# Two of four pairs of heads of the third half transposed by DMA instead of TensorE, with three reorderings around it

## The chip, the cores and the metric

The kernel runs on one core of a Trainium2 chip. The core has a matrix engine (TensorE, PE in the profile; its weight loads are listed apart as PEld), a vector engine (VectorE, DVE), an engine for activation functions and copies (ScalarE, ACT), a general engine (GpSimd, POOL) and an engine that here only issues transfers (SyncE, SP). Transfers run on 16 DMA engines; SP and POOL each keep a queue of them. The metric is the time of one execution on the device in microseconds, less is better. It is given as the median of several runs.

## The reference

The computation is attention with a limited window, followed by a gated feed-forward layer. `q`, `k` and `v` are 4 batches x 8 heads x 768 positions x 64 values, all float32.

```python
scores = scale * np.matmul(q, k.transpose(0, 1, 3, 2))
is_global = pos[None, :] < n_global                    # 8
is_local = (rel >= 0) & (rel < n_local)                # 96
dist = np.where(is_global & ~is_local, n_local, np.abs(rel))
bias = -slopes[:, None, None] * dist
a = softmax(np.where(is_global | is_local, scores + bias, -1e9))
x = np.matmul(a, v)            # then 3072 tokens x 512 (8 heads side by side)
out = (np.maximum(x @ w_gate, 0.0) * (x @ w_val)) @ w_out
```

A query sees the first 8 positions and the last 96 up to itself. `w_gate` and `w_val` are 512 x 1536, `w_out` is 1536 x 512. So there are two products of 512 x 1536 per token and one of 1536 x 512, and these are most of the arithmetic.

## The kernel before, in words

**Tiling.** The work is cut into 8 halves: half `s` is batch `s // 2` and half `s % 2` of its 768 positions, so 384 queries (`QH`). "Third half" in this document is `s = 2`, the first half of the second batch. In each half the 8 heads form four pairs `p` (`HP`), two heads of 64 values filling 128 rows. The keys of a batch form 7 tiles of 128 columns: 8 global keys and 120 others, so that one product yields scores against both. A pair's scores of one half fill three groups of columns. The feed-forward layer has 12 blocks of 128 columns (`N_FC`); its weights lie in SBUF in three groups of four blocks: `wg[0..2]`, `wv[0..2]`, and `wo_sb` for `w_out`.

**Steps of a half.** Keys and queries come with 128 positions on the rows of SBUF, and the scores need the 64 values there, so they are transposed first. Then come scores (PE), exponential (ACT), multiplication with a mask that holds the bias and the window (DVE), the product with v (PE), the logarithm and exponential that make a reciprocal (ACT, tiles `lnd` and `rcp`) and the multiplication into `xT` (DVE). The feed-forward follows, for each block `fc`: a gate product of four matmuls (one per quarter `dc` of the 512 inputs), a relu on ACT (`grelu`), a value product of four matmuls, and on DVE the product of both into `ht`. The output products read `ht` and `wo_sb`.

**Three ways of transposing.** Halves 0 and 1 are transposed by TensorE: `piece_t` (L288) multiplies with the identity, six or twelve matmuls at L299 per pair, into a PSUM bank; `piece_copy_k` (L304, copies at L278 to L280) and a copy of the queries bring them to SBUF. For half 1 the load itself casts to bfloat16 (`kc`, `qc`). Halves 3 to 7 use transfers: `early_pieces` (L378) has POOL cast keys and queries into `kc`/`qc` (`piece_cast2`), SP issue three DMA transposes each (`piece_x`, one per third `n` of the positions, all four pairs at once), and POOL put the keys into their tiles (`piece_order`, three copies per pair). Half 2 stands between: POOL casts (`cast(2, p, P, P)`, L979, from the loaded `ks`, `qs`), TensorE transposes, DVE makes three copies for the keys and ACT one for the queries (`T2_piece`, L982).

**The order of the work.** [...] The first part, up to the end of half 1's attention, is written out line by line. After it, `weave` (L813) emits a list of feed-forward items and puts other pieces between them: a piece with place 0.55 is emitted once 55% of the items' weight is out, and `spread` (L808) lays a list evenly between two places. `F0[2*i]` is the gate of block `i` of half 0 and `F0[2*i+1]` its value product. The first weave (L988) holds the blocks of half 1 and the rest of half 0's second group, with the third half's transposes among them; it runs from about 32.6 to 47.0 us. The second (L994) holds the last group of blocks, the output products of halves 0 and 1, the attention of the third half, the transposes of half 3 and the sums of `w_out` (`sums_wo`, DVE); it runs from 47.0 to 75.7 us.

**Buffers and queues.** Feed-forward products take turns in 3 PSUM banks (`ff_ps`), scores and the third half's transposes in 3 (`qk_ps`), products with v in 2 (`av_ps`). POOL issues the loads of weights and of v and those of `kc`/`qc`; SP issues the loads of later keys and queries, the copies that spread v's global rows over the seven tiles (`spread_v_globals`, L144), the DMA transposes and the stores. Weights and the third half's keys and queries are requested together at L923 to L926 in this order: `wg[1]`, `wv[1]`, `wg[2]`, `wv[2]`, keys, queries, `wo_sb`.

```python
weave(f1_1[G[0]] + f1_0[G[1]][4:] + f1_1[G[1]],
      ...
      spread(T2, 0.55, 0.95))
```

Of the kernel before, what the change touches and what calls it, by code (L numbers as in the profile page):

```python
# [16 lines left out]
def kernel(  # L17
# [12 lines left out]
    nc = tc.nc  # L30

    B, H, S, D = q.shape
# [6 lines left out]
    HP = H // 2  # L39
    QH = S // 2  # L40
    NN = 3
# [13 lines left out]
    for half in range(2):  # L55
# [33 lines left out]
    kNb = [const.tile([128, HP, QH], BF16, name=f"kN{i}") for i in range(2)]  # L89

    qT2 = [qTb[1].rearrange("d p e t -> d (p e t)")[:, i * HP * QH : (i + 1) * HP * QH].rearrange(
        "d (p t) -> d p t", p=HP) for i in range(2)]
    qc = [const.tile([128, NN, DM], BF16, name=f"qc{i}") for i in range(2)]
    kc = [const.tile([128, NN, DM], BF16, name=f"kc{i}") for i in range(2)]
# [16 lines left out]
    qs_of, ks_of = {}, {}  # L111

    def load_qk(s, h0, h1, eng=nc.sync):
        b, half = divmod(s, 2)
        if s not in qs_of:
            qs_of[s] = stage.tile([128, H, NN * D], FP32, name="qs")
            ks_of[s] = stage.tile([128, H, NN * D], FP32, name="ks")
        for src, dst in ((k, ks_of[s]), (q, qs_of[s])):
            eng.dma_start(
                out=dst[:, h0:h1, :],  # L120
                in_=src[b, h0:h1, half * QH : (half + 1) * QH, :].rearrange(
                    "h (p n) d -> p h (n d)", n=NN))
# [17 lines left out]
    def load_v_globals(b):  # L140
        nc.gpsimd.dma_start(out=v_dst(b, 0, NG, 0),
                            in_=v[b, :, 0:NG, :].rearrange("h p d -> p h d"))

    def spread_v_globals(b, j0=1, j1=NT):  # L144
        for j in range(j0, j1):
            nc.sync.dma_start(out=v_dst(b, 0, NG, j), in_=v_dst(b, 0, NG, 0))
# [5 lines left out]
    def load_v(b, j, r0=0, r1=KT):  # L152
        n = min(r1, S - KT * j) - r0
        nc.gpsimd.dma_start(  # L154
            out=v_dst(b, NG + r0, NG + r0 + n, j),
            in_=v[b, :, KT * j + r0 : KT * j + r0 + n, :].rearrange("h p d -> p h d"))
# [5 lines left out]
    def load_v_half(s):  # L162
        b, half = divmod(s, 2)
        if half == 0:
            load_v_globals(b)
            spread_v_globals(b)
        for j in range(4) if half == 0 else range(4, NT):
            load_v(b, j)

    def load_w(dst, src, f0, f1):  # L170
        nc.gpsimd.dma_start(out=dst, in_=src[:, f0:f1].rearrange("(c p) f -> p c f", p=128))

    def load_w_group(i):
        load_w(wg[i], moe_w_gate, i * GW * 128, (i + 1) * GW * 128)
        load_w(wv[i], moe_w_val, i * GW * 128, (i + 1) * GW * 128)
# [91 lines left out]
    def put_keys(copy, copy_small, kt, src, half):  # L267

        tk = src.rearrange("d (n p) -> d p n", n=NN)

        def put(j0, j1, p0, r0, r1):
            o = kt[:, j0:j1, r0:r1].rearrange("d j (p n) -> d j p n", n=NN)
            np_ = (r1 - r0) // NN
            i_ = tk[:, p0 : p0 + (j1 - j0) * np_, :].rearrange("d (j p) n -> d j p n", j=j1 - j0)
            return o, i_

        if half == 0:
            copy(*put(0, 3, 0, NG, 128))  # L278
            copy_small(*put(3, 4, 120, NG, NG + 24))
            copy_small(kt[:, :, 0:NG], kt[:, 0:1, NG : 2 * NG].to_broadcast([128, NT, NG]))  # L280
        else:
            copy(*put(4, 6, 32, NG, 128))
            copy_small(*put(3, 4, 0, NG + 24, 128))
            copy_small(*put(6, 7, 112, NG, NG + 48))
# [3 lines left out]
    def piece_t(s, p, pool=av_psum, name="av_ps", apart=False):  # L288
        for i in (1, 0):
            if i == 1 or apart:  # L290
                tp = pool.tile([128, 512], FP32, name=name)
                tp = tp[:, 0:QH].bitcast(BF16).rearrange("d (i t) -> d i t", i=2)
            tp_of[s, p, i] = tp[:, i, :]
            for n in range(NN):
                for e in range(2 if s == 1 else 1):
                    r = slice(64 * e, 64 * e + 64) if s == 1 else slice(0, 128)
                    src = (qk16[s, i][:, 2 * p + e, n * D : (n + 1) * D] if s == 1
                           else cast_of[s, p][:, i, n])
                    nc.tensor.matmul(tp[r, i, n * 128 : (n + 1) * 128],  # L299
                                     lhsT=src, rhs=ident, is_transpose=True,  # L300
                                     start=((i == 1 or apart) and n == 0),
                                     stop=((i == 0 or apart) and n == NN - 1))

    def piece_copy_k(s, p):  # L304
        b, half = divmod(s, 2)
        put_keys(nc.vector.tensor_copy, nc.vector.tensor_copy, kT[b % 2][p], tp_of[s, p, 1], half)

    def piece_copy(s, p):
        piece_copy_k(s, p)
        piece_copy_q(s, p)  # L310

    def piece_copy_q(s, p, copy=nc.vector.tensor_copy):
        for e in range(2):
            r = slice(64 * e, 64 * e + 64)
            copy(qTb[s % 2][r, p, e, :], tp_of[s, p, 0][r, :])
# [50 lines left out]
    def piece_cast2(s, p, dst, src):  # L366
        nc.gpsimd.tensor_copy(  # L367
            dst[s % 2].rearrange("t n (h d) -> t h n d", d=D)[:, 2 * p : 2 * p + 2],
            src[s][:, 2 * p : 2 * p + 2, :].rearrange("t e (n d) -> t e n d", n=NN))

    def piece_x(dst, src, n):
        nc.sync.dma_start_transpose(out=dst[:, :, n * 128 : (n + 1) * 128], in_=src[:, n])

    def piece_order(s, p):
        b, half = divmod(s, 2)
        put_keys(nc.gpsimd.tensor_copy, nc.gpsimd.tensor_copy, kT[b % 2][p], kNb[s % 2][:, p], half)
# [9 lines left out]
    def piece_qk(s, p, g, later=None):  # L386
        b, half = divmod(s, 2)
        kt = kT[b % 2][p]
        qd = qTb[s % 2][:, p].rearrange("d e (n p) -> d e n p", n=NN)
        bank = banks_of_half[half][g]  # L390
        cols = sum(2 * NN * w for _, _, w, _ in bank)
        ps = qk_psum.tile([128, 512], FP32, name="qk_ps")
        es = es_pool.tile([128, 480], BF16, name="es")
        c = 0
        for j, a, w, m in bank:
            n_ = 2 * NN * w
            nc.tensor.matmul(ps[:, c : c + n_], lhsT=kt[:, j, :],
                             rhs=qd[:, :, :, a : a + w], start=True, stop=True)
            c += n_
        nc.scalar.activation(es[:, 0:cols], ps[:, 0:cols], AF.Exp, bias=0.0, scale=scale)  # L400
        if later is None:
            piece_mask(s, p, bank, es)
        else:
            later.append(lambda: piece_mask(s, p, bank, es))
# [88 lines left out]
    def piece_mul_wide(s, p):  # L493
        if s not in xT_of:
            xT_of[s] = xt_pool.tile([128, N_DC, QH], BF16, name="xT")
        nc.vector.tensor_tensor(xT_of[s][:, p, :], av_of[s, p][1][:, 0:QH], av_of[s, p, "r"], op=ALU.mult)
# [311 lines left out]
    def spread(items, first, last, n=None):  # L808

        n = n or len(items)  # L810
        return [(first + (i + 0.5) / n * (last - first), f) for i, (_, f) in enumerate(items)]
# [22 lines left out]
    F0 = [f for _, f in f1_0]  # L834
# [86 lines left out]
    piece_biased(1, 0)  # L921
    load_v(0, 3, 24)
    load_w_group(1)  # L923
    load_w_group(2)
    load_qk(2, 0, H, nc.gpsimd)
    load_w(wo_sb, moe_w_out, 0, DM)  # L926
    for f in gate[0:3]:
        f(0, LAST)
    for f in gate[0:3]:
        f(LAST, N_DC)  # L930
    piece_t(1, 2)
    piece_t(1, 3)
    masks = {p: [] for p in (1, 2)}
    for g in range(3):
        piece_qk(1, 1, g, masks[1])
    piece_copy(1, 2)
    gate[3]()
    piece_copy(1, 3)
# [25 lines left out]
    piece_inverse_wide(1, 2)  # L964
    piece_ln_wide(1, 3)
    piece_mul_wide(1, 2)
    F0[9]()
    piece_inverse_wide(1, 3)
    piece_mul_wide(1, 3)
    F0[10]()  # L970
    F0[11]()
    for p in range(HP):
        nc.gpsimd.memset(kT[1][p][:, 3, 32:128].bitcast(mybir.dt.uint32), 0)
# [1 line left out]
    nc.gpsimd.memset(vbuf[1][:, NT - 1, :].bitcast(mybir.dt.uint32), 0)  # L975
    for j in range(NT):
        fill_ones(nc.gpsimd, 1, j)
    for p in range(HP):
        cast(2, p, P, P)  # L979
    load_v_half(2)  # L980

    def T2_piece(p):  # L982
        piece_t(2, p, *QKB, apart=True)
        piece_copy_k(2, p)
        nc.scalar.copy(qT2[0][:, p], tp_of[2, p, 0])

    T2 = [(0.0, lambda p=p: T2_piece(p)) for p in range(HP)]
    weave(f1_1[G[0]] + f1_0[G[1]][4:] + f1_1[G[1]],  # L988
          [(0.05 + 0.06 * j, lambda j=j: fill_ones(nc.vector, 0, j)) for j in range(NT)],
          [(0.1 + 0.2 * i, lambda h=h: setup_mask(h)) for i, h in enumerate((0, 1, 6, 7))],  # L990
          [(0.6, lambda: load_qk(3, 0, H)), (0.6, lambda: load_v_half(3))],
          spread(T2, 0.55, 0.95))
    sums_wo = [(0.0, f) for i in (0, 3) for f in weight_sums(i, i + 3)]
    weave(f1_0[G[2]] + f1_1[G[2]] + f2_0 + f2_1,  # L994
          spread(attention_pieces(2), 0.02, 0.86, 30), spread(early_pieces(3), 0.1, 0.76),
          spread(sums_wo, 0.08, 0.4))

    for c in range(2, NHALF):
        placed = []
# [43 lines left out]
```

The softmax here doesn't subtract the row's maximum and nothing guards it: scores larger than these inputs give would overflow.

## Time and profile before

| What | Value |
|---|---|
| Median of 7 runs | 237.44 us (237.13 to 237.76) |
| The profiled execution | 237.74 us, of which 236.0 us is its span |
| PE busy | 228.8 us (97%) |
| DVE busy | 186.9 us (79%) |
| ACT busy | 146.1 us (62%) |
| POOL busy | 88.8 us (38%) |
| Read and written in HBM | 28.38 MB and 6.29 MB |

The span runs from the first to the last instruction; the time of the execution also has what lies before and after it. Busy shares are averages over stages with different limits, so they are read stage by stage. Here are the stretches that matter, from the profile's table of windows (for each engine the busy time in us; "DMA share" is the mean load of the 16 engines, where a value over 1 means that packets overlap on an engine):

| Stretch, us | PE | DVE | ACT | POOL | DMA share | GB/s |
|---|---|---|---|---|---|---|
| 0 to 23 | 19.62 | 17.46 | 19.84 | 20.63 | 1.33 | 178 |
| 23 to 32.6 | 9.54 | 7.05 | 8.26 | 6.53 | 1.36 | 202 |
| 32.6 to 47 (first weave) | 14.40 | 10.73 | 8.51 | 7.41 | 1.21 | 250 |
| 47 to 75.7 (second weave) | 28.70 | 24.72 | 16.71 | 14.87 | 1.02 | 158 |
| 75.7 to 200 | 124.08 | 103.15 | 82.05 | 39.39 | 0.55 | 118 |
| 200 to 236 | 32.49 | 23.78 | 10.72 | 0.00 | 0.13 | 45 |

The TensorE clock that was granted is 1.00 throughout. PE's ends are modelled, so its busy time says that it always had work queued, not that each matmul ran at its peak.

### The profile page before, as it was taken

To read this page: it belongs to the slowest core of one execution; us is meant where nothing else is said; L and a number is where in the kernel's file an instruction comes from. 1 tells how busy PE (TensorE), PEld (TensorE's weight loads), DVE (VectorE), ACT (ScalarE), POOL (GpSimd) and SP (SyncE) were. 2 spreads that over 40 slices of the span, in tenths; PEclk is the share of its full clock that TensorE was granted. 3 is DMA by queue.
4 is the path that set the end of the run, shared out by engine and by line. 5 is a ranking of instruction groups with operands and counts; after the bars stand their busy time and mean duration, and the time that the engine had idled before them with its cause. 6 is when DMAs were issued, how large, how long until landed. Compare 5 with 4: busy or idle time off the path is not lost.

```text
span 236.0 us, 5509 instructions
## 1 busy us (share of the span) xinstructions
PE 228.8 (97%) x2021; PEld 158.0 (67%) x2021; DVE 186.9 (79%) x466; ACT 146.1 (62%) x321; POOL 88.8 (38%) x191
## 2 busy tenths in 40 slices
PE   7889999999999999999999999999999999999994
PEld 3675666656678666856688666856679566865683
DVE  6868767769988789786999789886899779773784
ACT  7979875667624887467842787567842687624310
POOL 8998902942583066406580066405330000000000
PEclk9999999999999999999999999999999999999999
DMA  6999999998359856856397764846422200020005
GB/s 186 184 158 183 205 253 292 178 120 263 75 142 185 253 162 92 52 166 215 90 83 118 239 172 90 53 139 223 87 44 89 92 0 3 0 92 0 1 3 178
DMA packets 71420, 30.43 MB, mean 129 GB/s; under 512 B 47745, under 2 KB 70785, under 8 KB 71393
## 3 DMA queue, kind: packets, MB, share of 16 engines
q0 software_dynamic: 34896, 10.27, 38.9%
q1 hardware_dynamic: 36496, 19.82, 29.6%
q8 instruction: 16, 0.26, 0.5%
q14 instruction: 12, 0.09, 0.1%
HBM read 28.38 MB, written 6.29 MB: 147 GB/s over the span
## 4 chain that ended last, share of the span: by engine, by line
PE 86%; DVE 3%; POOL 3%; DMA 3%; ACT 2%; issue 1%; POOLq 0%; DVEq 0%; ACTq 0%
PE ff_ps L748 52%; PE ff_ps L634 20%; PE av_ps L431 6%; DMA kc<-in_q_dram 3%; PE ff_ps L781 2%; PE av_ps L515 2%; PE qk_ps L515 2%; POOL vbuf L154 1%; DVE obuf L647 1%; PE qk_ps L299 1%; PE av_ps L468 1%; ACT es L400 1%; ACT es L359 1%; PE qk_ps L468 1%; ACT grelu L757 0%
## 5 line engine op out<-in xcount | busy, mean ns | idle before, releaser
L757 ACT ACTIVATE grelu<-ff_ps 128x384 bf16<-128x384 f32 x96 | 46.7, 490 | 51.8 <-PE ff_ps L748 38.6
L748 PE MATMUL ff_ps<-xT,wv 128*128 128x384 bf16 x384 | 77.9, 326 | 0.0
L748 PE MATMUL ff_ps<-xT,wg 128*128 128x384 bf16 x384 | 77.8, 326 | 0.0
L764 DVE TENSOR_TENSOR ht<-ff_ps,grelu 128x384 f16<-128x384 f32 x96 | 53.3, 557 | 27.2 <-PE ff_ps L748 22.9
L748 PEld LDWEIGHTS <-wv 128*128 128x128 bf16 x384 | 36.0, 98 | 23.9 <-issue 1.4
L748 PEld LDWEIGHTS <-wg 128*128 128x128 bf16 x384 | 36.4, 97 | 21.2 <-issue 0.5
L647 DVE TENSOR_TENSOR obuf<-ff_ps,obuf 128x512 f32<-128x512 f32 (+1 forms) x46 | 27.6, 603 | 5.3 <-ACT rcp L446 2.2
L367 POOL CAST kc<-ks 128x384 bf16<-128x384 f32 x20 | 10.2, 552 | 54.1 <-DMA ks<-in_k_dram 54.1
L536 DVE TENSOR_TENSOR es<-es,m_all 128x432 bf16<-128x432 bf16 (+3 forms) x108 | 30.3, 324 | 0.2 <-ACT es L524 0.2
L453 DVE TENSOR_TENSOR xT<-av_ps,rcp 64x384 bf16<-64x384 f32 x48 | 26.5, 553 | 4.7 <-ACT rcp L446 4.0
L440 ACT ACTIVATE lnd<-av_ps 64x384 f32<-64x384 f32 x48 | 23.3, 485 | 11.1 <-PE av_ps L431 10.3
L524 ACT ACTIVATE es<-qk_ps 128x432 bf16<-128x432 f32 (+2 forms) x54 | 27.7, 532 | 0.0
L154 POOL DMA_DIRECT2D vbuf<-in_v_dram x29 | 24.8, 870 | 0.3 <-DVE hsum L630 0.3
L431 PEld LDWEIGHTS <-vbuf 128*128 128x128 bf16 x216 | 18.3, 98 | 4.7 <-DVE xT L453 0.4
L431 PE MATMUL av_ps<-es,vbuf 128*128 128x216 bf16 (+4 forms) x216 | 21.4, 226 | 0.0
L634 PEld LDWEIGHTS <-ht 128*128 128x128 f16 x198 | 18.6, 97 | 3.5 <-DVE ht L764 0.5
L634 PEld LDWEIGHTS <-hsum 128*128 128x128 f16 x192 | 18.5, 98 | 2.1
L634 PE MATMUL ff_ps<-wo_sb,ht 128*128 128x256 f16 x132 | 18.5, 272 | 0.2 <-DVE ht L764 0.2
L634 PE MATMUL ff_ps<-wo_sum,hsum 128*128 128x256 f16 x144 | 17.2, 273 | 0.0
L446 ACT ACTIVATE rcp<-lnd 128x384 f32<-128x384 f32 x24 | 12.6, 524 | 0.7
L524 ACT ACTIVATE es<-av_ps 128x432 bf16<-128x432 f32 (+2 forms) x18 | 9.5, 528 | 1.8 <-PE qk_ps L515 1.8
L515 PEld LDWEIGHTS <-kT 64*128 64x128 bf16 x216 | 6.6, 94 | 5.9 <-issue 3.8
(130 smaller groups left out, 264.2 us busy)
## 6 DMA issues: line engine op xcount, KB each, us to landing
out_dram<-obuf SPq DMA_DIRECT2D x22, 256.0 KB
ks<-in_k_dram SPq DMA_DIRECT2D x5, 768.0 KB
qs<-in_q_dram SPq DMA_DIRECT2D x5, 768.0 KB
vbuf<-in_v_dram POOLq DMA_DIRECT2D x23, 120.0 KB, 4.7
wv<-in_moe_w_val_dram POOLq DMA_DIRECT2D x3, 512.0 KB, 10.1
wo_sb<-in_moe_w_out_dram POOLq DMA_DIRECT2D x1, 1536.0 KB, 21.7
wg<-in_moe_w_gate_dram POOLq DMA_DIRECT2D x2, 512.0 KB, 10.0
ks<-in_k_dram SPq DMA_DIRECT2D x4, 192.0 KB
```

The source lines that it names most:

```text
L154: nc.gpsimd.dma_start(out=v_dst(b, NG + r0, NG + r0 + n, j), in_=v[b, :, KT * j + r0 : KT * j + r0 + n, :].rearrange("h p d -> p h d"))
L431: nc.tensor.matmul(av3[:, :, a : a + w], lhsT=vb[:, j, z0 : z0 + 128], rhs=es[:, c : c + NN * w].rearrange("k (n p) -> k n p", n=NN), star ...
L440: nc.scalar.activation(ln[o0 : o0 + 64], av[d0 : d0 + 64, 0:QH], AF.Ln, bias=0.0, scale=1.0)
L453: nc.vector.tensor_tensor(xT_of[s][r, p, :], av_of[s, p, e][r, 0:QH], av_of[s, p, "r"][r], op=ALU.mult)
L515: nc.tensor.matmul(banks[e][:, c : c + NN * w], lhsT=kT[b % 2][p][r, j, :], rhs=q3[:, :, a : a + w], start=True, stop=True)
L524: nc.scalar.activation(es[:, 0:cols], ps[:, 0:cols], AF.Exp, bias=0.0, scale=scale)
L536: nc.vector.tensor_mul(e4, e4, mk)
L634: nc.tensor.matmul(ps[:, c0 : c0 + DH], lhsT=lhs(i), rhs=rhs(i), start=(i == 0), stop=(i == NP - 1), skip_group_check=True)
L647: add = lambda o, x, y: nc.vector.tensor_tensor(o, x, y, op=ALU.add)
L748: nc.tensor.matmul(st[key][:, 0:QH], lhsT=w_of(w, dc, fc), rhs=xT_of[c][:, dc, :], start=(dc == 0), stop=(dc == N_DC - 1))
L757: nc.scalar.activation(gr, psg[:, 0:QH], AF.Relu, bias=0.0, scale=1.0)
L764: nc.vector.tensor_tensor(ht[:, fc, :], psv[:, 0:QH], st["r", fc], op=ALU.mult)
```

## The change

The change has six parts.

1. The third half's keys and queries are requested before `wg[2]` and `wv[2]` instead of after them.
2. The scores of half 1's pair 1 are put ahead of the transposes of half 1's pairs 2 and 3.
3. In the last part before the first weave, gate 5 of half 0 (`F0[10]`) comes ahead of value product 4 (`F0[9]`).
4. The third half's pairs 2 and 3 are cast by POOL into `kc[0]` and `qc[0]` (their half of the columns), transposed by six DMA transposes of two pairs' width on SP's queue (`piece_x` has a new parameter for the first pair), and put into their key tiles by POOL (`piece_order`), behind the issue of the v loads. Pairs 0 and 1 stay with `cast` and TensorE.
5. `T2` holds two pieces instead of four, spread over places 0.65 to 0.95 instead of 0.55 to 0.95.
6. The sums of `w_out` begin at place 0.1 instead of 0.08.

```diff
-    def piece_x(dst, src, n):
-        nc.sync.dma_start_transpose(out=dst[:, :, n * 128 : (n + 1) * 128], in_=src[:, n])
+    def piece_x(dst, src, n, p=0):
+        nc.sync.dma_start_transpose(out=dst[:, p:, n * 128 : (n + 1) * 128], in_=src[:, n, 128 * p :])
...
     load_w_group(1)
+    load_qk(2, 0, H, nc.gpsimd)
     load_w_group(2)
-    load_qk(2, 0, H, nc.gpsimd)
     load_w(wo_sb, moe_w_out, 0, DM)
...
-    piece_t(1, 2)
-    piece_t(1, 3)
     masks = {p: [] for p in (1, 2)}
     for g in range(3):
         piece_qk(1, 1, g, masks[1])
+    piece_t(1, 2)
+    piece_t(1, 3)
...
     piece_mul_wide(1, 2)
-    F0[9]()
+    F0[10]()
     piece_inverse_wide(1, 3)
     piece_mul_wide(1, 3)
-    F0[10]()
+    F0[9]()
     F0[11]()
...
-    for p in range(HP):
+
+    for to, src in ((kc, ks_of), (qc, qs_of)):
+        for p in (2, 3):
+            piece_cast2(2, p, to, src)
+        for n in range(NN):
+            piece_x((kNb if to is kc else qT2)[0], to[0], n, 2)
+    for p in (0, 1):
         cast(2, p, P, P)
     load_v_half(2)
+    for p in (2, 3):
+        piece_order(2, p)
...
-    T2 = [(0.0, lambda p=p: T2_piece(p)) for p in range(HP)]
+    T2 = [(0.0, lambda p=p: T2_piece(p)) for p in range(2)]
...
-          spread(T2, 0.55, 0.95))
+          spread(T2, 0.65, 0.95))
...
-          spread(sums_wo, 0.08, 0.4))
+          spread(sums_wo, 0.1, 0.4))
```

## Prediction

> **What bounds the kernel now.** I read the page first: busy shares, the 40 slices, the chain that ended last.
>
> ```profile
> span 236.0 us, 5509 instructions
> PE 86%; DVE 3%; POOL 3%; DMA 3%; ACT 2%; issue 1%; POOLq 0%; DVEq 0%; ACTq 0%
> PE ff_ps L748 52%; PE ff_ps L634 20%; PE av_ps L431 6%; DMA kc<-in_q_dram 3%; PE ff_ps L781 2%; PE av_ps L515 2%; PE qk_ps L515 2%; POOL vbuf L154 1%; DVE obuf L647 1%; PE qk_ps L299 1%; PE av_ps L468 1%; ACT es L400 1%; ACT es L359 1%; PE qk_ps L468 1%; ACT grelu L757 0%
> ```
>
> TensorE (PE) is the path for 86% of the span. Next came the chain in order of time, cut to 10 to 60 us (start, length, what).
>
> ```profile
> 20.57 1.14 ACT grelu L757 x3
> 21.71 1.35 ACT es L400 x3
> 23.06 0.04 issue
> 23.10 0.34 PE qk_ps L397
> 23.44 1.30 PE ff_ps L748 x8
> ...
> 40.59 0.41 PE qk_ps L299 x6
> ...
> 45.57 0.34 PE qk_ps L299 x6
> ```
>
> From 17.8 to 23.06 us ScalarE (ACT) leads; from 23.10 it is PE without a break, so beyond that point a microsecond of PE work removed is a microsecond gained, and a wait added on PE is lost. The two L299 pieces are the first and the last of the third half's four groups of transposes, one per pair of heads; the two between, at 42.30 and 43.93, take 0.34 each. The timeline of the 30.6 to 34.3 us stretch shows the other edited place (start, duration, instruction, count; in brackets idle time before it):
>
> ```profile
> 30.67 0.82 PE L748 MATMUL ff_ps<-xT,wv 128*128 128x384 bf16 x4
> 30.80 0.47 ACT L485 ACTIVATE lnd<-qk_ps 128x384 f32<-128x384 f32 x1
> 31.30 0.52 ACT L490 ACTIVATE rcp<-lnd 128x384 f32<-128x384 f32 x1
> 31.33 0.81 PE L748 MATMUL ff_ps<-xT,wg 128*128 128x384 bf16 x4
> 31.53 0.56 DVE L764 TENSOR_TENSOR ht<-ff_ps,grelu 128x384 f16<-128x384 f32 x1
> 32.00 0.55 DVE L496 TENSOR_TENSOR xT<-qk_ps,rcp 128x384 bf16<-128x384 f32 x1
> 32.18 0.49 ACT L757 ACTIVATE grelu<-ff_ps 128x384 bf16<-128x384 f32 x1 [0.36 <-PE ff_ps L748]
> 33.28 0.81 PE L748 MATMUL ff_ps<-xT,wv 128*128 128x384 bf16 x4
> ```
>
> A group of four matmuls starts every 0.65 us here and its modelled end is 0.16 us after the next one's start. Nothing on PE waits; ACT and VectorE (DVE) have a few tenths to spare.
>
> **What the Trainium skill says.** "TensorE: Matmul & The Clock Gate", section "Architectural detail: the array is 16× 32×32, not 1× 128×128": the queues of ACT and DVE are strict FIFO. So an instruction put ahead of a ready one delays it. The lines above agree: gate 5's relu (32.18) stands behind rcp and nothing overtakes. The same page, "Part 4: PE-mode transpose": a transpose on TensorE lands in PSUM and needs a copy after it; the trace has them (DVE L278 to L280, ACT L985). "DMA: Bandwidth & Descriptors", "Anatomy of one DMA — SWDGE (gpsimd) path": a DMA's semaphore wait is held by the issuing sequencer. POOL shows it at 22.93 us, where the issue of wv[2] stood 1.03 us until wv[0] had landed. The same page, "Queues, rings and completion order": each DMA engine takes turns between the queues that have work. No run here shows transposes beside weight loads; that is my largest unknown.
>
> **The change, part by part**, against the profiled execution: 237.74 us, of which 236.0 is span and 1.74 lies around it.
>
> *Two pairs leave TensorE.* Twelve matmuls at L299 go, two groups of 0.34 us in the chain (six starts 0.056 apart): 2 × 0.335 = -0.67. Six DVE copies (2 × (0.52 + 0.17 + 0.22) us) and two ACT copies (2 × 0.48) go as well; worth nothing, since both engines idle 0.4 us and more between their instructions there.
>
> *The keys and queries of the third half are loaded ahead of wg[2] and wv[2].* Landings, from issue plus time to landing: wv[1] 30.4, wg[2] 33.0, wv[2] 36.1, ks 38.0, qs 40.05, wo_sb 47.5. Two 512 KB weight halves move behind: ks lands about 30.4 + 1.9 = 32.3, qs 34.3, wg[2] 36.9, wv[2] 40, wo_sb as before. wg[2] is first used at 47.0 and wv[2] at 47.7, over 7 us later. The issue of qs now stands where wv[2] stood, waiting for wv[0] until 22.9; behind it on POOL are wg[2], wv[2], wo_sb and memsets, none early. POOL's casts, waiting 8.2 us for ks now, end near 37 rather than 43.3. The first transpose group at 40.43 (0.41 instead of 0.34) no longer waits for a cast: -0.06.
>
> *What the transfers add.* POOL casts as before (0.51 each). SyncE (SP) issues six transposes from about 33.4; three of four pairs' width took 3.82 us at 85.35, so three of half width take between 1.9 and 3.8: all issued by 37.5 to 41. On POOL the pairs' six key copies (0.53 + 0.20 + 0.23, twice, 1.9 us) stand behind the five v issues (0.62 + 4 × 0.87) and ahead of three more; they end near 43.5. First use is the second score group of the next stage at 52.3: over 8 us of cover. SP's row copies for v (47.81, waiting for v's global rows) are queued behind the transposes, but were waiting 42.9 us anyway. Taken: nothing on the path. Cost to DMA: three full-width transposes with what went beside them gave a share of 0.30 over 3.9 us at 85.3, that is 1.2 us of the engines; six of half width cost 1.2, or 2.4 if it goes by the piece. The queue is full at that time (share 1.12 from 36 to 40), so wo_sb lands 1.2 to 2.4 us later, at 48.7 to 49.9. wo_sb is first read by DVE at 51.26; v's rows follow it, and their row copies for the third key tile are issued as third of six 0.81 us steps, at 49.4 to 50.25, land perhaps 1.5 us later (transposes issued by 64.49 released POOL at 65.83), and are read at 54.9: 3.1 us of cover. Cost 0, ends 0 and +0.5.
>
> *Gate 5 ahead of value product 4.* wv[1] landed at 30.4, PE needs it at 30.67: there is no wait to remove in this execution. It costs, though. In the new order, ACT has relu 5 between lnd and rcp, and DVE has xT of pair 3 ahead of ht 4. Gate 5 runs from 30.67, ends 31.49; relu 31.53 to 32.02; rcp 0.52 more, overlapped by 0.07: 32.47; xT 32.50 to 33.05; ht 4, overlapped 0.08, 32.97 to 33.53. With three ff_ps banks, the value product at 33.28 takes the bank that ht 4 frees (in the old order it was one that a relu had freed at 32.67). With 0.05 for the signal it starts at 33.59: +0.31. Ends: +0.2 and +0.4; 0 if ordinary runs do wait for wv[1].
>
> *Scores of pair 1 ahead of the transposes of pairs 2 and 3.*
>
> ```profile
> 20.04 0.86 PE L299 MATMUL av_ps<-ident,kc 128*64 128x128 bf16 x24
> 20.61 0.41 DVE L282 COPY kT<-av_ps 128x240 bf16<-128x240 bf16 x1 [0.47 <-PE av_ps L299]
> 21.56 1.49 ACT L400 ACTIVATE es<-qk_ps 128x480 bf16<-128x480 f32 x3
> 22.22 1.22 PE L397 MATMUL qk_ps<-qT,kT 128*128 128x144 bf16 x5
> ```
>
> The transposes ran as soon as PE was free (kc's queries landed at 20.06, needed at 20.2). Moved first, the scores wait for their own inputs: the q copy ends 20.14, the third bank's exponential 20.57; they run from 20.19 to 20.80. ACT takes them at 21.56 either way, so nothing is gained. The transposes start near 20.90, DVE's copies of pair 2 begin 0.57 later (as 20.04 to 20.61) and end 1.31 after that, at 22.78. Pair 2's scores start at 22.83 instead of 22.22; the last of them, which waited for ACT until 23.10, goes at 23.23: +0.13. DVE is then 0.85 us late, inside the 1.44 us it idles before 28.02. Ends: -0.1 (if kc is later than in this execution) and +0.2.
>
> *Sums 0.08 to 0.1, the transposes' places 0.65 to 0.95.* DVE's work in that stage is the same and starts at the same point; the eight sums move one instruction later at most, and every product's wait on DVE had 0.35 us or more between release and start: 0.
>
> Sum: -0.67 - 0.06 + 0.31 + 0.13 = -0.29, so 237.45 for the profiled execution. That one stands 0.30 above the median of 7 (237.44), near the top; carried over, 237.15.
>
> **The rivals.** A: the sum, own range 236.7 to 237.5. B: the two reorderings cost nothing, because ordinary executions get kc and wv[1] later than this one. For: the margins were 0.14 and 0.27 us. Against: spread of the runs is only 0.6 us. Then -0.67 - 0.06 - 0.1 = -0.83: 236.6. C, the slower side: the transposes hold up the full queue of weights. v's row copies come late and the first product with v of the third half (54.7) stalls PE. It decides from 3.1 us of delay; at 4.6, if a transpose blocks an engine for about its 0.65 to 1.27 us of issue (six: 3.9 to 7.6), the stall is 1.5 and the sum +1.2: 238.65. Against: a share of only 0.30 while transposes run. D: PE time is freed, but the next stage, where DVE is busy 11.9 of 12 us from 52 to 64, sets the pace and takes it back: 0, 237.4. Against: no product waits for DVE there now.
>
> **How the numbers follow.** A change under 0.2% (0.47 us) is what a measurement here can't tell from none. A has 0.45: its term of 0.31 may be smaller, so 0.17 of it lies beyond 0.47 faster, 0.26 inside, 0.02 slower. B 0.32: 0.31 faster, 0.01 inside. C 0.17, slower. D 0.06, inside. Faster 0.48, same 0.33, slower 0.19. The range goes from below B (236.3) to the near part of C (238.2); about 0.06 is left below, 0.13 above.
>
> **What would show it.** Right: two L299 groups left in the chain after 40 us; the value product near 33.6 starting on ht's release; PE at its first value product near 23.4; POOL's key copies long before the second scores. Wrong: no gap near 33.3 (B), PE waiting at v's products or DVE at the first sum (C), or new gaps before L748 between 52 and 64 (D).

## The result, and the profile after

The changed kernel took 238.58 us (median of 14 runs, 237.77 to 239.3), against 237.44 us before. The ratio of the two is 1.0044, with a 95% interval of 1.003 to 1.0057: slower by 0.7 to 1.35 us. The recorded ratio is not the quotient of the two medians, which is 1.0048 and lies within the interval. The prediction had 237.15 us, with a range from 236.3 to 238.2. The measured time is on the side of rival C (238.65 us), to which the prediction gave 0.17. Executions over 1.5% above the fastest of the same kernel (three of v_ahead, one of transfers_only) are left out of all medians and ratios here.

The profiled execution of the changed kernel took 237.99 us. From its page, the span, and the chain that ended last by engine and by line:

```profile
span 236.2 us, 5487 instructions
PE 74%; DMA 16%; POOL 6%; issue 1%; DVE 1%; POOLq 0%; DVEq 0%
PE ff_ps L748 42%; PE ff_ps L634 20%; PE av_ps L431 6%; DMA vbuf<-in_v_dram 5%; DMA ks<-in_k_dram 5%; DMA wv<-in_moe_w_val_dram 4%; PE ff_ps L781 2%; DMA vbuf<-vbuf 2%; PE av_ps L515 2%; PE qk_ps L515 1%; POOL vbuf L154 1%; POOL kc L131 1%; DVE obuf L647 1%; POOL obuf L263 1%; POOL wg L171 1%
```

Transfers have grown from 3% to 16% of the chain, and PE has fallen from 86% to 74%. The chain in order of time says where (start, length, what):

```profile
36.90 12.54 DMA vbuf<-in_v_dram
49.46 4.83 DMA vbuf<-vbuf
54.28 0.14 issue
54.42 0.59 PE av_ps L431 x3
55.01 1.31 PE ff_ps L748 x8
```

Up to 54.3 us PE no longer leads. The chain comes through two transfers: v's eight global rows, 12.54 us from issue to landing, and the copies of these rows to the other tiles, 4.83 us from the first issue until the first of them is there. Then PE goes on. The timeline of PE at the third half's first products with v (L431), after:

```profile
53.57 0.26 PE L431 MATMUL av_ps<-es,vbuf 128*128 128x216 bf16 x1
54.42 0.59 PE L431 MATMUL av_ps<-es,vbuf 128*128 128x216 bf16 x3 [0.59 <-DMA vbuf<-vbuf]
```

and before:

```profile
54.70 0.42 PE L431 MATMUL av_ps<-es,vbuf 128*128 128x216 bf16 x4
```

PE reaches the first of four products 1.13 us earlier than before (53.57 against 54.70), then stands before the second, third and fourth, one for each key tile whose rows are copied. Against the spacing of before that is 0.76 + 0.12 + 0.14 = 1.02 us. Of the 1.13 us, 0.64 had been there at the first value product (22.64 against 23.28) and come from this execution's own earlier start; the stretch from there on, in which two groups of transposes are gone, gave 0.49.

The queues show what came late. First the issues on SP's queue from 20 to 60 us, after, then before:

```profile
33.24 3.85 SPq L372 DMA_TRANSPOSE kN<-kc  x3
37.25 3.74 SPq L372 DMA_TRANSPOSE qT<-qc  x3
49.46 4.51 SPq L146 DMA_DIRECT2D vbuf<-vbuf  x6
54.10 0.39 SPq L119 DMA_DIRECT2D ks<-in_k_dram  x1
```

```profile
47.81 4.88 SPq L146 DMA_DIRECT2D vbuf<-vbuf  x6
52.89 0.38 SPq L119 DMA_DIRECT2D ks<-in_k_dram  x1
```

The row copies start 1.65 us later, because v's global rows landed at 49.44 instead of 47.74. These stand behind `wo_sb` on POOL's queue. From the view of the transfers between 8 and 60 us, the hardware queue (packets, MB, share of the 16 engines) and the issue of `wo_sb` (the last number is us from issue to landing), before and then after:

```profile
q1 hardware_dynamic: 2513, 1.62, 10.7%
...
wo_sb<-in_moe_w_out_dram POOLq DMA_DIRECT2D x1, 1536.0 KB, 21.7
```

```profile
q1 hardware_dynamic: 4133, 1.94, 16.2%
...
wo_sb<-in_moe_w_out_dram POOLq DMA_DIRECT2D x1, 1536.0 KB, 23.8
```

By the trace's packets, from 38 to 44 us POOL's queue moved 216 KB per us before and 160 after, while the transposes took a share of 0.30 of the engines beside it. With the loads in the new order and no transposes (orders_only, below) it is 208. The six landed at 39.4, 41.3, 43.1, 45.0, 47.2 and 48.75: about 1.85 us each, although SP had issued the last by 41.0. The Trainium skill, "DMA: Bandwidth & Descriptors", "Queues, rings and completion order", states that a DMA engine takes turns between the queues that have work. The trace agrees as far as it shows rates: with two queues at work from 38 to 44 us, the weights lost a quarter of theirs.

### The profile page after: what moved, and what is told of

It reads as the page before. It is cut to its first block, busy times and chain, and to the rows that moved or that the text cites. A ratio compares the mean times of both kernels' runs of the same rounds, so it can differ in the third digit from the quotient of the medians.

```text
span 236.2 us, 5487 instructions
## 1 busy us (share of the span) xinstructions
PE 228.4 (97%) x2009; PEld 157.0 (66%) x2009; DVE 186.9 (79%) x460; ACT 145.0 (61%) x319; POOL 90.7 (38%) x197
## 4 chain that ended last, share of the span: by engine, by line
PE 74%; DMA 16%; POOL 6%; issue 1%; DVE 1%; POOLq 0%; DVEq 0%
PE ff_ps L748 42%; PE ff_ps L634 20%; PE av_ps L431 6%; DMA vbuf<-in_v_dram 5%; DMA ks<-in_k_dram 5%; DMA wv<-in_moe_w_val_dram 4%; PE ff_ps L781 2%; DMA vbuf<-vbuf 2%; PE av_ps L515 2%; PE qk_ps L515 1%; POOL vbuf L154 1%; POOL kc L131 1%; DVE obuf L647 1%; POOL obuf L263 1%; POOL wg L171 1%
## 5 line engine op out<-in xcount | busy, mean ns | idle before, releaser
L764 DVE TENSOR_TENSOR ht<-ff_ps,grelu 128x384 f16<-128x384 f32 x96 | 53.2, 556 | 26.9 <-PE ff_ps L748 23.3
L367 POOL CAST kc<-ks 128x384 bf16<-128x384 f32 x22 | 11.4, 558 | 56.2 <-DMA ks<-in_k_dram 53.5
L536 DVE TENSOR_TENSOR es<-es,m_all 128x432 bf16<-128x432 bf16 (+3 forms) x108 | 31.3, 335 | 0.2 <-ACT es L524 0.2
L431 PE MATMUL av_ps<-es,vbuf 128*128 128x216 bf16 (+4 forms) x216 | 21.8, 226 | 0.6 <-DMA vbuf<-vbuf 0.6
L431 PEld LDWEIGHTS <-vbuf 128*128 128x128 bf16 x216 | 18.2, 98 | 5.8 <-issue 1.0
L367 POOL CAST qc<-qs 128x384 bf16<-128x384 f32 x22 | 11.3, 555 | 1.7 <-DMA qs<-in_q_dram 1.7
```

What stands on the lines that cost most here:

```text
L367: nc.gpsimd.tensor_copy(dst[s % 2].rearrange("t n (h d) -> t h n d", d=D)[:, 2 * p : 2 * p + 2], src[s][:, 2 * p : 2 * p + 2, :].rearrange ...
L431: nc.tensor.matmul(av3[:, :, a : a + w], lhsT=vb[:, j, z0 : z0 + 128], rhs=es[:, c : c + NN * w].rearrange("k (n p) -> k n p", n=NN), star ...
L536: nc.vector.tensor_mul(e4, e4, mk)
L764: nc.vector.tensor_tensor(ht[:, fc, :], psv[:, 0:QH], st["r", fc], op=ALU.mult)
```

## The experiments

Two theories. Q (queue): the transposes delay `wo_sb`, v's global rows and their copies, and PE waits for these. O (orders): the two reorderings cost more than forecast, and the wait at v is a small matter. All ratios below are to the kernel before, measured again beside each third of the table (237.53, 237.64 and 237.55 us), with 95% intervals. With few runs a ratio can stand apart from the quotient of the medians: for after_again, on 9 runs, the quotient is 1.0028. "The wait at v" is PE's wait at the third half's first four products at L431, against the spacing of before; where it is 0, the profile shows no wait, though in most of these runs the four lie 0.12 us further apart than in before.

| Run | Median us | Ratio | Interval | Wait at v in its profile, us |
|---|---|---|---|---|
| after_again | 238.19 | 1.0054 | 1.0027 to 1.0081 | 0.81 |
| orders_only | 237.66 | 1.0009 | 0.9997 to 1.0022 | 0 |
| transfers_only | 238.56 | 1.0042 | 1.0026 to 1.0059 | 0.87 |
| v_ahead | 238.84 | 1.0058 | 1.0037 to 1.0079 | 1.05 (fourth product) |
| v_ahead_qk3 | 237.06 | 0.9980 | 0.9968 to 0.9992 | 0 |
| v_ahead_qk3_old | 236.55 | 0.9952 | 0.9933 to 0.9971 | 0 |
| before_v_ahead | 238.21 | 1.0028 | 1.0014 to 1.0043 | 0 |
| keys_only | 236.90 | 0.9969 | 0.9957 to 0.9981 | 0 |
| rows_by_pool | 240.01 | 1.0108 | 1.0087 to 1.0129 | 0 (0.43 for a mask) |
| rows_split | 237.90 | 1.0018 | 1.0006 to 1.0031 | 1.70 |
| keys_gate_old | 236.98 | 0.9984 | 0.9971 to 0.9996 | 0 |
| v_ahead_qk3_gate_old | 237.08 | 0.9978 | 0.9964 to 0.9993 | 0 |

### after_again: the changed kernel once more

> The changed kernel once more, for a second profile. Theory Q (queue): the six transposes take turns with the weight loads, so wo_sb and behind it v's global rows land 1.7 us later than before; the row copies of v land 4 to 5 us after their issue, and PE stands at its second to fourth product with v of the third half until they do. Expected: this wait again, 0.7 us or more, ending at 54.3 us or later, and what follows it as long as before. Theory O (orders): the score and gate reorderings lengthen PE's path before 34 us by 0.8 us or more, and the wait at v is small (under 0.3 us).

The wait came again, 0.56 + 0.11 + 0.14 = 0.81 us. It also showed a second one. PE's waits between 17 and 80 us in this execution (engine, line, for what: us, times, longest):

```profile
PE av_ps L431 <- DVE xT L453: 0.4, 1, 0.4
PE av_ps L431 <- DMA vbuf<-vbuf: 0.4, 1, 0.4
PE qk_ps L397 <- DVE qT L315: 0.3, 1, 0.3
```

The first line is at 66.45 us: another product with v waits for DVE's normalisation of the pair before, which frees its PSUM bank. From one matmul's start to the next it costs 0.58 us; in the first profile of the changed kernel it was 0.15, and in before nothing. DVE was late for this reason (DVE's timeline, 61.5 to 66.6 us; POOL's below it):

```profile
62.30 0.85 DVE L628 TENSOR_TENSOR hsum<-hsum,ht 128x768 f16<-128x768 f16 x1
63.08 0.68 DVE L536 TENSOR_TENSOR es<-es,m_all 128x432 bf16<-128x432 bf16 x1
63.68 0.85 DVE L629 TENSOR_TENSOR hsum<-ht 128x768 f16<-128x768 f16 x1
64.46 0.85 DVE L630 TENSOR_TENSOR hsum<-ht,hsum 128x768 f16<-128x768 f16 x1
...
65.86 1.13 DVE L453 TENSOR_TENSOR xT<-av_ps,rcp 64x384 bf16<-64x384 f32 x2
```

```profile
59.26 2.89 POOL L367 CAST kc<-ks 128x384 bf16<-128x384 f32 x4 [9.05 <-DMA ks<-in_k_dram]
62.10 2.80 POOL L367 CAST qc<-qs 128x384 bf16<-128x384 f32 x4
```

Three of the sums take 0.85 us and a mask 0.68. In the kernel before, the same four take 0.55 and 0.37, and POOL's casts for the fourth half end at 62.35 (DVE, then POOL, before):

```profile
62.51 0.55 DVE L628 TENSOR_TENSOR hsum<-hsum,ht 128x768 f16<-128x768 f16 x1
62.97 0.37 DVE L536 TENSOR_TENSOR es<-es,m_all 128x432 bf16<-128x432 bf16 x1
63.27 0.55 DVE L629 TENSOR_TENSOR hsum<-ht 128x768 f16<-128x768 f16 x1
63.74 0.55 DVE L630 TENSOR_TENSOR hsum<-ht,hsum 128x768 f16<-128x768 f16 x1
```

```profile
59.84 2.51 POOL L367 CAST qc<-qs 128x384 bf16<-128x384 f32 x4
```

In after_again they run until 64.90: the keys they read are requested behind the row copies on SP's queue (54.1 instead of 52.9). The Trainium skill, "SBUF — State Buffer", "Who interferes with whom", states that a DVE instruction with two inputs in SBUF contends with a GpSimd instruction that reads SBUF, and that one with at most one input in SBUF does not, outside certain faster modes. The trace agrees with both: the sums and the mask are longer beside a cast, and `ht` at L764, with one input in PSUM, took 0.54 us beside one.

### orders_only and transfers_only: the two halves of the change

orders_only puts all four pairs back on TensorE and keeps the requests, the scores, the gate and the sums as changed:

```diff
-    for to, src in ((kc, ks_of), (qc, qs_of)):
...
-    for p in (0, 1):
+    for p in range(HP):
         cast(2, p, P, P)
     load_v_half(2)
-    for p in (2, 3):
-        piece_order(2, p)
...
-    T2 = [(0.0, lambda p=p: T2_piece(p)) for p in range(2)]
+    T2 = [(0.0, lambda p=p: T2_piece(p)) for p in range(HP)]
...
-          spread(T2, 0.65, 0.95))
+          spread(T2, 0.55, 0.95))
```

> Parts 1, 2, 3 and 6 of the change (requests, scores first, gate 5 first, sums), with all four pairs on TensorE as before. Theory Q: no wait at the products with v; 0.26 us for the gate and -0.3 to +0.2 for the scores, so 237.3 to 237.9, ratio 0.9995 to 1.002. Theory O: the loss is here: 238.3 to 238.7, ratio 1.004 to 1.0055.

transfers_only keeps the transfers and puts the scores and the gate back:

```diff
+    piece_t(1, 2)
+    piece_t(1, 3)
     masks = {p: [] for p in (1, 2)}
     for g in range(3):
         piece_qk(1, 1, g, masks[1])
-    piece_t(1, 2)
-    piece_t(1, 3)
...
-    F0[10]()
+    F0[9]()
     piece_inverse_wide(1, 3)
     piece_mul_wide(1, 3)
-    F0[9]()
+    F0[10]()
```

> Parts 1, 4, 5 and 6 (requests, transposes by transfers, two places), with scores and gate in the order of before. Theory Q: the time ends at the row copies of v, so it is 238.2 to 238.8 (ratio 1.003 to 1.006), with PE waiting 0.9 us or more at them. Theory O: 0.67 us of transposes are gone and nothing is added: 236.6 to 236.9, ratio 0.997.

The loss is in the transfers: 1.0042 alone, 1.0009 without them. O falls. With the reorderings or without them the transfers cost the same: the first row copy lands at 54.27 us in transfers_only and at 54.28 in the changed kernel, so the end of the wait is set by the transfers and not by when PE arrives. In the profile of transfers_only PE also waited 0.5 us for `kc`'s queries at 20.1.

### v_ahead: v's global rows ahead of wo_sb

```diff
     load_w_group(2)
-    load_w(wo_sb, moe_w_out, 0, DM)
...
         fill_ones(nc.gpsimd, 1, j)
+    load_v_globals(1)
+    load_w(wo_sb, moe_w_out, 0, DM)
...
-    load_v_half(2)
+    spread_v_globals(1)
+    for j in range(4):
+        load_v(1, j)
```

> The changed kernel with v's global rows of the second batch requested ahead of wo_sb, so that their row copies go right behind the transposes on SP and land near 49 us. Theory Q: the wait at the products with v is gone, and 0.67 + 0.06 of transposes less 0.26 of the gate remain: 236.7 to 237.2, ratio 0.997 to 0.999. Theory O: no change from the changed kernel: 238.4, ratio 1.004.

A miss: it was as slow as the changed kernel. The three needed row copies did land early, at 49.0 to 49.4, but PE waited at the fourth product (24 columns, tile 3) instead, and for another transfer:

```profile
55.49 0.10 PEld L431 LDWEIGHTS <-vbuf 128*128 128x128 bf16 x1 [1.18 <-DMA vbuf<-in_v_dram]
55.50 0.19 PE L431 MATMUL av_ps<-es,vbuf 128*128 128x24 bf16 x1 [0.89 <-DMA vbuf<-in_v_dram]
```

On SP's queue the loads of the fourth half's keys and queries, 768 KB each, had been held back by the row copies. Now they were issued at 47.01 and 48.61 and took turns with v's own loads, of which the fourth landed at 55.45 instead of 52.6. The wait that was removed had been a gate for something larger.

### v_ahead_qk3 and v_ahead_qk3_old: the gate put back in another place

```diff
-          [(0.6, lambda: load_qk(3, 0, H)), (0.6, lambda: load_v_half(3))],
+          [(0.6, lambda: load_v_half(3)), (0.6, lambda: load_qk(3, 0, H, nc.gpsimd))],
```

> As v_ahead, and the keys and queries of the fourth half are loaded from POOL's queue behind v's loads, so that they cannot take turns with v's loads. Theory Q: neither row copies nor v's loads are late at the first products with v (wait under 0.15 us), POOL's casts for the fourth half come at 56 to 61 us, and the time is 236.7 to 237.3, ratio 0.997 to 0.999. If a wait at v is not what costs the time, it stays at 238.3 or more, ratio 1.003 or more.

v_ahead_qk3_old has the same two edits on top of transfers_only.

> The same with the scores and gate 5 in the order of before. Theory Q: 0.26 us of the gate are gone too: 236.4 to 237.0, ratio 0.9955 to 0.998. If the reorderings are worth something, it is slower than v_ahead_qk3.

In both, the wait at v is gone and the casts come at 57.7 to 62.7 us. With nothing else changed in what is transposed where, the ratio goes from 1.0044 to 0.998. v_ahead_qk3_old has the lowest ratio of all, 0.9952, but on 6 runs, and its interval overlaps that of v_ahead_qk3. It was not slower than v_ahead_qk3, so the reorderings showed no worth here.

The profiled execution of v_ahead_qk3 (238.07 us, among the slowest of its 22) has a wait of another kind:

```profile
76.59 0.81 PE L748 MATMUL ff_ps<-xT,wg 128*128 128x384 bf16 x4 [0.80 <-DVE obuf L647]
```

From start to start it costs 0.96 us. Neither v_ahead_qk3_old nor v_ahead_qk3_gate_old has it in its profile, and its cause stays open.

### before_v_ahead: the same two edits without the change

The edits of v_ahead_qk3, made to the kernel before.

> The kernel before with only v's global rows ahead of wo_sb and the fourth half's loads on POOL's queue. It has no wait at v to remove, so theory Q says no change: ratio 0.999 to 1.001. If the two moves are worth something by themselves, it is faster by 0.3 us or more.

A miss, and on the slower side: 1.0028. Nothing waited at v, before or now, but the fourth half's keys arrived earlier, and POOL's casts with them, from 55.05 us. DVE and PE from 55.5 to 60 us:

```profile
58.31 0.85 DVE L600 TENSOR_TENSOR wo_sum<-wo_sb,wo_sum 128x768 f16<-128x768 f16 x1
59.09 1.13 DVE L453 TENSOR_TENSOR xT<-av_ps,rcp 64x384 bf16<-64x384 f32 x2
...
59.69 0.26 PE L515 MATMUL av_ps<-qT,kT 64*128 64x216 bf16 x1 [0.80 <-DVE xT L453]
```

Again sums of 0.85 us and a normalisation that frees a bank too late. So the casts hurt here when they are early as well as late. In the kernel before they also lengthen instructions of DVE (0.86, 0.83 and 0.68 us between 57.8 and 62.6), but no wait of PE follows. Whether this is the whole loss is not shown: the profile also has a wait of 0.4 us for `kc`'s queries near 20 us. It does mean that the gain of v_ahead_qk3 is not from its two edits by themselves.

### keys_only: half as many transposes

```diff
-    for to, src in ((kc, ks_of), (qc, qs_of)):
-        for p in (2, 3):
-            piece_cast2(2, p, to, src)
-        for n in range(NN):
-            piece_x((kNb if to is kc else qT2)[0], to[0], n, 2)
+    for p in (2, 3):
+        piece_cast2(2, p, kc, ks_of)
+    for n in range(NN):
+        piece_x(kNb[0], kc[0], n, 2)
     for p in (0, 1):
         cast(2, p, P, P)
+    for p in (2, 3):
+        piece_cast(2, p, 0, P)
...
+    def T2_queries(p):
+        tp = qk_psum.tile([128, 512], FP32, name="qk_ps")[:, 0:QH].bitcast(BF16).rearrange("d (i t) -> d i t", i=2)
+        for n in range(NN):
+            nc.tensor.matmul(tp[:, 0, n * 128 : (n + 1) * 128], lhsT=cast_of[2, p][:, 0, n], rhs=ident,
+                             is_transpose=True, start=(n == 0), stop=(n == NN - 1))
+        nc.scalar.copy(qT2[0][:, p], tp[:, 0, :])
...
-    T2 = [(0.0, lambda p=p: T2_piece(p)) for p in range(2)]
+    T2 = [(0.0, lambda p=p: (T2_piece if p < 2 else T2_queries)(p)) for p in range(HP)]
...
-          spread(T2, 0.65, 0.95))
+          spread(T2, 0.55, 0.95))
```

> The changed kernel with transfers for the keys of the two pairs alone, their queries on TensorE: three transposes instead of six. Theory Q: v's global rows land about 0.9 us later than before instead of 1.7 (near 48.5), the row copies at 53.2 to 53.5, so PE hardly waits at v (under 0.3 us); 0.34 us of transposes are saved and 0.26 paid for the gate: 237.2 to 237.8, ratio 0.999 to 1.001. If the number of transposes does not matter, the wait is as in the changed kernel and the time 238.3 or more.

Issues on SP's queue, and PE at the products with v:

```profile
48.08 4.51 SPq L146 DMA_DIRECT2D vbuf<-vbuf  x6
52.77 0.40 SPq L119 DMA_DIRECT2D ks<-in_k_dram  x1
```

```profile
53.67 0.54 PE L431 MATMUL av_ps<-es,vbuf 128*128 128x216 bf16 x4
```

v's global rows landed at 48.07, the three needed row copies at 53.25, 53.46 and 53.66, just in time. PE waited for nothing from 24 to 80 us. At 0.9969 (236.9 us) it is faster than expected, and beats the kernel before by more than the 0.34 us of transposes explains; what else it gains was not found. The delay grows with the number of transposes, counted from orders_only (rows at 47.31): 0.76 us for three, 2.13 for six.

### rows_by_pool: late rows, quick copies

```diff
-    load_v_half(2)
+    load_v_globals(1)
+    for j in range(4):
+        load_v(1, j)
     for p in (2, 3):
         piece_order(2, p)
+    copy_v_globals(P, 1, 1, 4)
+    copy_v_globals(P, 1, 4, NT)
...
-          [(0.6, lambda: load_qk(3, 0, H)), (0.6, lambda: load_v_half(3))],
+          [(0.6, lambda: load_v_half(3)), (0.6, lambda: load_qk(3, 0, H, nc.gpsimd))],
```

> The changed kernel with v's global rows put into tiles 1 to 6 by two copies on POOL instead of six row copies on SP's queue (and the fourth half's keys and queries on POOL's queue behind v's loads, as in v_ahead_qk3). v's global rows still land at 49.4, as late as in the changed kernel. If their lateness alone makes the wait, it stays; if it is the 4.6 to 5.2 us that the row copies need from there, it goes: the copies take some 1.8 us each, so tiles 1 to 3 are complete near 51.5, ahead of PE at 53.7. Then 236.7 to 237.4, ratio 0.997 to 0.9995; else 238.3 or more.

A miss, and the slowest of all, but not for v's sake: the rows were there at 51.3, as expected, and no wait for `vbuf` was left. But (timeline from 49 to 54.2 us):

```profile
49.83 3.02 POOL L150 COPY vbuf<-vbuf 8x1536 bf16<-8x1536 bf16 x2 [4.53 <-DMA vbuf<-in_v_dram]
...
49.98 3.10 DVE L536 TENSOR_TENSOR es<-es,m_all 128x432 bf16<-128x432 bf16 x2
...
54.07 0.32 PE L748 MATMUL ff_ps<-xT,wg 128*128 128x384 bf16 x1 [1.50 <-DVE ht L764]
```

Two masks that take 0.37 us alone took 1.55 and 1.64 beside POOL's two copies on eight partitions (1.46 and 1.61 us). DVE fell behind by 2.4 us, and PE waited 1.67 us for it at 54.07 and 0.8 us at 68.03. The lateness of the rows alone does not make the wait; the way they are spread decides, and in this kernel POOL is the wrong way.

### rows_split: the casts earlier, the wait at v left as it is

```diff
-    load_v_half(2)
+    load_v_globals(1)
+    spread_v_globals(1, 1, 4)
+    load_qk(3, 0, H)
+    spread_v_globals(1, 4, NT)
+    for j in range(4):
+        load_v(1, j)
...
-          [(0.6, lambda: load_qk(3, 0, H)), (0.6, lambda: load_v_half(3))],
+          [(0.6, lambda: load_v_half(3))],
```

> The changed kernel with the loads of the fourth half's keys and queries behind the third of the six row copies instead of behind the sixth, so issued near 51.8 instead of 54.1 us. Theory Q with its second part (late casts on POOL meet the four sums on DVE and delay it, PE waits again near 66 us): the wait at v stays (0.8 us or more), the casts come 1.5 to 2 us earlier, and the wait near 66 us falls under 0.1 us: 237.9 to 238.4, ratio 1.001 to 1.003. If the casts do not matter, the ratio stays 1.004 to 1.0055.

PE at the products with v, and POOL's casts:

```profile
53.51 0.26 PE L431 MATMUL av_ps<-es,vbuf 128*128 128x216 bf16 x1
...
55.06 0.58 PE L431 MATMUL av_ps<-es,vbuf 128*128 128x216 bf16 x3 [1.29 <-DMA vbuf<-vbuf]
```

```profile
57.38 2.34 POOL L367 CAST kc<-ks 128x384 bf16<-128x384 f32 x4 [6.69 <-DMA ks<-in_k_dram]
59.67 2.51 POOL L367 CAST qc<-qs 128x384 bf16<-128x384 f32 x4
```

The wait at v stayed, at 1.70 us in this profile, the casts ended at 62.2, and the wait near 66 us was gone. The ratio of 1.0018 lies where the second part of Q put it. By that, the late casts are some 0.6 us of the loss (1.0044 against 1.0018), but this is not clear of noise: the intervals just touch. Nor is the separation clean, for the loads that were put between the row copies come with a wait at v 0.7 us longer than the changed kernel's, in an execution 0.6 us above this run's median, and PE comes to the place near 66 us half a microsecond later than in the changed kernel. Against v_ahead_qk3, with neither the wait at v nor late casts (0.998), the wait is worth some 0.9 us, and those intervals do not meet.

### keys_gate_old and v_ahead_qk3_gate_old: the gate by itself

Both have gate 5 and value product 4 in the order of before (the second part of the diff of transfers_only) and the scores first.

> keys_only with gate 5 and value product 4 in the order of before, the scores still first. The gate's 0.26 us go, less the 0.15 us or so that PE may wait for wv[1]: 0.1 to 0.3 us faster than keys_only, ratio 0.9955 to 0.9967. If gate first is worth something, slower than keys_only.

> v_ahead_qk3 with gate 5 and value product 4 in the order of before, the scores still first. 0.1 to 0.3 us faster than v_ahead_qk3 (0.998), ratio 0.9965 to 0.9978; as the scores first gain 0.15 us or more, not slower than v_ahead_qk3_old (0.9952) beyond its interval. If v_ahead_qk3_old owed its lead to the old order of the scores, this one stays at 0.998.

0.9984 against 0.9969, a miss, and 0.9978 against 0.998: no gain from the old order, and by the first pair rather a loss, both within the intervals. In keys_gate_old PE lost 0.25 us at value product 4, which began at 30.85, 0.04 after `wv[1]` had landed. So the 0.26 us that gate first costs in a trace is about what it saves when `wv[1]` is not yet there. The second run stayed at 0.998, as expected if v_ahead_qk3_old owed its lead to the old order of the scores. That lead (0.9952 against 0.9978, some 0.6 us) rests on 6 runs, and the intervals overlap.

## Why the prediction was wrong, point by point

**The step that failed is "What the transfers add", in its last term: the cover of v's row copies.** It got most of the rest right. Measured beside its estimates: keys at 32.1 (32.3), queries at 34.1 (34.3), casts done at 37.0 (near 37), six transposes issued by 41.0 (37.5 to 41), key copies done at 44.9 (43.5), `wo_sb` at 49.3 (48.7 to 49.9). The transposes took 3.2 us of the 16 engines' time by their packets, where it had 1.2 or 2.4. Then it put the row copies' landing at "perhaps 1.5 us" after issue, with the transposes of half 3 as the nearest row, and got "3.1 us of cover. Cost 0, ends 0 and +0.5". In fact a row copy took 4.2 to 4.3 us before and 3.6 to 4.8 after, while v's loads fill the other queue: before, issued from 47.81, the three needed ones landed at 52.09, 53.08 and 53.78. The cover of the last was 54.95 - 53.78 = 1.2 us, not 3.1. In the changed kernel it landed 0.9 us later, at 54.70, and PE came 1.1 us earlier; the other two were late as well. These landings stood in the trace of before. A second term is missing: what stands behind the row copies on SP's queue, the fourth half's keys and queries, and with them POOL's casts, which meet DVE's sums.

**The saving itself was right, and was given back.** From the first value product of half 0 to the first product with v of the third half PE took 31.42 us before and 30.93 after: -0.49, where the prediction's terms for this stretch, -0.67 - 0.06 + 0.31, give -0.42. It is 31.60 in orders_only, so the transposes alone are 0.67.

**Gate 5 ahead.** In a trace, +0.26 at the value product, 32.90 us, against +0.31 forecast, and through the steps that were named (from the timeline after):

```profile
31.28 0.51 ACT L490 ACTIVATE rcp<-lnd 128x384 f32<-128x384 f32 x1
31.82 0.56 DVE L496 TENSOR_TENSOR xT<-qk_ps,rcp 128x384 bf16<-128x384 f32 x1 [0.99 <-ACT rcp L490]
...
32.30 1.01 DVE L764 TENSOR_TENSOR ht<-ff_ps,grelu 128x384 f16<-128x384 f32 x2
...
32.90 0.81 PE L748 MATMUL ff_ps<-xT,wv 128*128 128x384 bf16 x4
```

The steps show the order of ACT's queue, too: `rcp`, whose input was ready at 30.62, stood behind relu 5, for which ACT idled 0.26 us. (The line that the prediction took for this, the relu at 32.18, was waiting for PE.) Over many runs gate first costs nothing that can be told, as the two gate_old runs show. The prediction named that end ("0 if ordinary runs do wait for wv[1]") and did not take it.

**Scores ahead.** Forecast +0.13, with +0.2 as its upper end. ACT leads here, so it is measured from the start of ACT's exponentials for half 1's pair 0 (19.14 us before, 18.30 after) to the first value product (23.28 and 22.64): 4.14 us before and 4.34 after, so +0.20. It is 4.15 in v_ahead_qk3_old, with the old order, and 4.30 to 4.34 in five more profiles with the new one. In the others a load comes late. With the old order, in transfers_only and before_v_ahead, the queries in `kc` did, and it took 4.82 and 4.70. With the new order, in rows_split, rows_by_pool, v_ahead_qk3 and keys_gate_old, it took 4.45 to 4.96, and the first value product began 0.04 or 0.05 us after `wv[0]` had landed. In the two with the old order `wv[0]` landed at 22.62 and 22.58, with the first value product at 22.88 and 22.76, so the new order could have gained 0.2 us there at most; the forecast had put that end at -0.1. Over many runs its cost is not settled: orders_only has next to none, and the lead of v_ahead_qk3_old would make it 0.6 us.

**The rivals.** B, that the reorderings cost nothing, was true of them (orders_only: 1.0009) and did not decide. C had the right place and mechanism, v's row copies and the first product with v. Its point of decision was wrong: not "from 3.1 us of delay" but from about 1. Its chance of 0.17 rested on that number. That its 238.65 us lies so near the measured 238.58 is luck: it had a delay of 4.6 us and a stall of 1.5, where v's rows came 1.65 us later and the stall was 0.8 to 1.0, and it had no late casts. D, that DVE takes the freed time back in the next stage, was right in part: the wait near 66 us is a DVE wait, 0.15 and 0.58 us in two profiles. It goes with POOL's later casts; PE comes to that stage only 0.11 and 0.24 us earlier than before (63.11 and 62.98 against 63.22), so its earlier arrival does not make the second.

**The sum again.** By stretches, +0.20 (scores) - 0.49 (to the products with v) + 1.02 (wait at v) + 0.15 (wait near 66 us) is +0.88 us in the first profile of the changed kernel, and +0.16 - 0.49 + 0.81 + 0.58 = +1.06 in the second; measured +0.7 to +1.35. That these agree so well is in part luck. The same count gives +0.50 for orders_only (measured +0.2), +0.17 for keys_only (-0.7) and +1.53 for rows_split (+0.4), so one profile against one is good to about 1 us. The profiled executions of the two kernels differ by 0.25 us alone, mainly because ACT came to half 1's exponentials 0.84 us earlier in that of the changed kernel, ahead of everything that the change touches.

## What to carry to other kernels

A step that is moved from an engine to transfers is paid for in the queues: ask what is behind it in every queue, how long that took to land in the trace of before, and who reads it first. The time from issue to landing must be read for the transfer in question and in its own traffic; here copies of 8 KB beside a full queue took 4 us and more. And where a wait in a queue is taken away, look for what it was holding back: here first a larger load, then casts that lengthened VectorE's instructions.

## What the runs showed of the hardware that was not expected

- Six row copies of 8 KB each, SBUF to SBUF, took 4.3 to 5.3 us from the issue of the first to its landing while POOL's queue was full (before, after and seven of the runs), and in the traces of before and after hardly a packet moved in the first 2.5 us. In the four runs where transposes still stood ahead of them on SP's queue it was 7.7 to 7.9 us, and the first landed 0.2 to 0.5 us after the last transpose. Why was not settled.
- DMA transposes of two pairs' width took as long to issue, 3.85 us for three, as those of four pairs' width in the kernel before (3.82 us for three), and landed about 1.85 us apart beside the weight loads.
- A POOL copy on eight partitions, 1.46 us long, came with a mask multiplication on DVE four times as long as alone (1.55 us for 0.37).
